# Whole-tensor loads and whole chunks for every batch of a gated recurrence and its mixer

## The chip, the cores and the metric

One core of a Trainium2 chip runs the kernel. The metric is the device time of one execution in microseconds; the number quoted for a kernel is the median of its runs.

## The reference

Four batches, eight heads, a sequence of 768 and a head size of 48; all inputs and the output are float32. First a gated linear recurrence for each batch and head:

```python
for t in range(S):
    state = alpha[:, :, t, :, None] * state + np.einsum('bhd,bhe->bhde', k[:, :, t], v[:, :, t])
    y[:, :, t] = np.einsum('bhd,bhde->bhe', q[:, :, t], state)
```

Its result, with the heads side by side (x of 768 x 384 for each batch), goes through a mixer of low rank along the sequence, and then through an MLP of width 1536:

```python
h = xt @ U @ V                     # xt: x transposed; U 768x32, V 32x768
u = x + h.transpose(0, 2, 1)
ch = np.maximum(u @ w_ch1, 0.0) @ w_ch2
return (u + ch)
```

The mixer mixes over the whole sequence. So the MLP of a batch can begin only when the recurrence of that batch is complete.

## The kernel before

**The recurrence in chunks.** The sequence of a batch is cut into pieces of 128 rows, the partitions. For each piece the kernel takes the logarithm of alpha (`lt`, on ACT), sums it along the rows by a matmul with a triangular matrix (`f_cum`), takes the exponent of the sum with either sign (`ai`, `aa`, `tot`), scales k and q by these (`rk`, `rq`; `f_scale`), transposes both on TensorE (`f_tr`) and evacuates them (`kT`, `qT`; `f_ev`), multiplies them into scores (`f_sc`), masks these (`pm`; `f_mask`), and forms y from the masked scores and `rv` (v in bf16) and from `qT` and the state that the pieces before have left (`f_y`). The state itself is carried on by `f_d`, an addition and `f_st`.

**Two layouts.** Batch 3 is done by `stage_gla`: a piece is a chunk of 128 consecutive positions of all eight heads, and there are six of them. The batches in `PAIR = (0, 1, 2)` are done by `stage_pair`: a piece is 256 positions of four heads, in which a partition holds two neighbouring positions. That makes the contiguous pieces of a load 2 x 48 floats, 384 B, where a chunk of batch 3 has 48 floats, 192 B. In a pair unit the sums take two more matmuls (L385, L386), and scores, states and y are made in halves of 64 rows (L445, L479, L531), so with more and smaller matmuls. `stage_pair` may put `f_scale` on DVE or on POOL, `stage_gla` on POOL only.

**Mixer and MLP.** `stage_mix` makes x times U (`utx`), adds h to x (`ub`, L713) and makes the transposed `uT`; `mlp1` (L749) makes `h1` from `uT` and the first weights, in two halves of the sequence; `mlp2` (L772) makes the output of a chunk from `h1` and the second weights; DVE adds `ub` (L779) and SP stores 192 KB (L780).

**Loads.** All transfers are issued by SP, in one queue. `load` in `stage_loads` brings 192 KB at a time (L342 for pairs, L349 for chunks of batch 3), into one of 36 buffers of the pool `io`, which the 24 tiles of float32 weights (L317, then cast to bf16 on POOL or ACT) use too. `U` and `V` have places of their own.

**Order.** No engine chooses at run time: the class `Plan` collects all operations with what they read and write, the engines that can do them, a cost in ns and a priority, and plays them through once while the program is being built. Out of that comes the order in which each engine's queue is written. A load has a cost for SP (750 for a pair tile, 1000 for a chunk, 540 for a weight tile). A buffer (`Buf`) takes a slot of its pool when its first operation is placed and gives it back after its last. The priority of a load is that of its batch and chunk (`b * NC + c` and a small offset); the first weights have 5.5, the second `W2AT = 7.9`. Operations of the recurrence have `(b * NC + c) * 100` and a few more, and those of the MLP of a batch come about three chunks after the recurrence of the next has begun (`mlp_prio`). While TensorE waits during the first 28 us of the plan, matmuls on zeros are put in (`P.warm`, "filler").

Of the kernel before, what the change touches and what calls it, by code (L numbers as in the profile page):

```python
# [8 lines left out]
FP32 = mybir.dt.float32  # L9
BF16 = mybir.dt.bfloat16  # L10
AF = mybir.ActivationFunctionType
# [3 lines left out]
class Pool:  # L15

    def __init__(self, slots):
        self.slots = list(slots)
        self.free = [0.0] * len(self.slots)


class Buf:
# [10 lines left out]
    def __call__(self):  # L33
        return self.slot
# [140 lines left out]
def mm(*cols):  # L175
    return sum(max(c / 2.4 + 2.5, 25.0) for c in cols)
# [3 lines left out]
def kernel(  # L180
# [24 lines left out]

    const = ctx.enter_context(tc.tile_pool(name="const", bufs=1))
# [15 lines left out]
    u_sb = const.tile([128, NC, R], BF16, name="u_sb")  # L222
    vm_sb = const.tile([128, S], BF16, name="vm_sb")
# [23 lines left out]
    sel = const.tile([R, 4, R], BF16, name="sel")  # L247
# [48 lines left out]
    def copy(eng, dst, src):  # L296
        if eng == "ACT":
            nc.scalar.copy(dst, src)  # L298
        elif eng == "DVE":
            nc.vector.tensor_copy(dst, src)  # L300
        else:
            nc.gpsimd.tensor_copy(dst, src)  # L302

    def small():
        P.add({"SP": 450.0}, lambda e: nc.sync.dma_start(u_in, moe_U.rearrange("(c p) r -> p c r", p=128)), w=["u_in"], prio=2.5)
        P.add({"SP": 500.0}, lambda e: nc.sync.dma_start(v_in, moe_V), w=["v_in"], prio=2.5)
        P.add({"POOL": 300}, lambda e: nc.gpsimd.tensor_copy(u_sb, u_in), r=["u_in"], w=["u"], prio=395)
        P.add({"POOL": 800}, lambda e: nc.gpsimd.tensor_copy(v_bf, v_in), r=["v_in"], w=["v_bf"], prio=396)
        for i in range(2):
            vb = Buf(bank)  # L310
            sl = slice(i * TW, (i + 1) * TW)
            P.add({"PE": mm(TW)}, lambda e, vb=vb, sl=sl: nc.tensor.matmul(vb()[:, 0:TW], lhsT=sel.rearrange("r a b -> r (a b)"), rhs=v_bf[:, sl], start=True, stop=True), r=["v_bf"], w=[vb], prio=397, mode="V")
            P.add({"DVE": 470, "ACT": 390}, lambda e, vb=vb, sl=sl: copy(e, vm_sb[:, sl], vb()[:, 0:TW]), r=[vb], w=[("vm", i)], prio=398)

    def weight(dst, src, key, prio, pr, engs):
        t = Buf(io)
        P.add({"SP": 540.0}, lambda e: nc.sync.dma_start(flat(t), src), w=[t], prio=prio)  # L317
        P.add(engs, lambda e: copy(e, dst, flat(t)), r=[t], w=[key], prio=pr)

    def flat(t):  # L320
        return t().rearrange("p h d -> p (h d)")
# [12 lines left out]
    tiles = {}  # L334

    def stage_loads(b):
        def load(t, src, c, key):
            if b in PAIR:
                hs, sl = slice((c % 2) * HP, (c % 2 + 1) * HP), slice((c // 2) * 2 * C, (c // 2 + 1) * 2 * C)
                P.add(  # L340
                    {"SP": 750.0},
                    lambda e: nc.sync.dma_start(  # L342
                        t().rearrange("p (h j) d -> p h (j d)", j=2), src[b, hs, sl, :].rearrange("h (p j) d -> p h (j d)", j=2)
                    ),
                    w=[t], prio=key,
                )
                return
            sl = slice(c * C, (c + 1) * C)
            P.add({"SP": 1000.0}, lambda e: nc.sync.dma_start(t(), src[b, :, sl, :].rearrange("h t d -> t h d")), w=[t], prio=key)  # L349

        for c in range(NC):
            at, qt, kt, vt = (Buf(io) for _ in range(4))
            tiles[b, c] = at, qt, kt, vt
            kk = b * NC + c
            for t, src, o in ((at, alpha, -0.7 if c else 0.0), (kt, k, 0.1), (qt, q, 0.2), (vt, v, 1.25 if c < NC - 1 and b in PAIR else 0.3)):
                load(t, src, c, kk + o)

    def xk(b, xb, c):
        return [(xb, c, 0), (xb, c, 1)] if b in PAIR else [(xb, c)]

    def stage_pair(b, u, sprev, xb):

        blk, half = u // 2, u % 2
        pr = (b * NC + u) * 100.0
        sl = 0.0 if b == 0 else 150.0
        at, qt, kt, vt = tiles[b, u]

        def raw(t):
            return t().rearrange("p (h j) d -> p j h d", j=2)

        def jh(x):
            return x.rearrange("p (j h) d -> p j h d", j=2)

        lt = Buf(lts)
        P.add({"ACT": 435}, lambda e: nc.scalar.activation(jh(lt()[:, :, 0:D]), raw(at), AF.Ln), r=[at], w=[lt], prio=pr + 40, slack=sl)  # L375
        rv = Buf(rvs)
        P.add({"POOL": 480, "ACT": 420}, lambda e: copy(e, jh(rv()), raw(vt)), r=[vt], w=[rv], prio=pr + 20, slack=sl)

        cb = Buf(bank)
        Q = HP * D  # L380
# [16 lines left out]
        aa, ai, tot = Buf(aas), Buf(ais), Buf(tots)  # L397
# [10 lines left out]
        P.add(both, lambda e: f_scale(e, rk, kt, ai), r=[kt, ai], w=[rk], prio=pr + 10, slack=sl)  # L408
        P.add(both, lambda e: f_scale(e, rq, qt, aa), r=[qt, aa], w=[rq], prio=pr + 11, slack=sl)

        tk, tq = Buf(bank), Buf(bank)
        kT, qT = Buf(kts), Buf(qts)
# [54 lines left out]
        def sview(x):  # L467
            return x[0]()[:, 2 * x[1] : 2 * x[1] + 2, :].rearrange("p a d -> p (a d)")
# [20 lines left out]
        for c in range(nch):  # L489
# [14 lines left out]
            else:  # L504
# [3 lines left out]
                    lambda e, c=c, sm=sm, prev=prev: nc.vector.tensor_tensor(sm()[:, 0:Q], db[c]()[:, 0:Q], sview(prev), op=ALU.add),  # L508
                    r=[db[c], prev], w=[sm], prio=pr + 4, slack=sl,
# [31 lines left out]
    def stage_gla(b, c, sprev, xb):  # L541
        kk = b * NC + c
        pr = kk * 100.0
        sl = 150.0
        at, qt, kt, vt = tiles[b, c]
        lt = Buf(lts)
        P.add({"ACT": 435}, lambda e: nc.scalar.activation(lt()[:, :, 0:D], at(), AF.Ln), r=[at], w=[lt], prio=pr + 40, slack=sl)
        rv = Buf(rvs)
        P.add({"POOL": 480}, lambda e: copy(e, rv(), vt()), r=[vt], w=[rv], prio=pr + 20, slack=sl)

        cb = Buf(bank)

# [11 lines left out]
        aa, ai, tot = Buf(aas), Buf(ais), Buf(tots)  # L564
# [10 lines left out]
        P.add(both, lambda e: f_scale(e, rk, kt, ai), r=[kt, ai], w=[rk], prio=pr + 10, slack=sl)  # L575
        P.add(both, lambda e: f_scale(e, rq, qt, aa), r=[qt, aa], w=[rq], prio=pr + 11, slack=sl)

        tk, tq = Buf(bank), Buf(bank)
        kT, qT = Buf(kts), Buf(qts)
# [41 lines left out]
        if c < NC - 1:  # L621
# [25 lines left out]
            else:  # L647
# [4 lines left out]
                    r=[db, sprev], w=[sm], prio=pr + 4, slack=sl,  # L652
# [112 lines left out]
    def mlp2(b, ub, h1, c):  # L765
# [13 lines left out]
        P.add({"DVE": 468}, lambda e: nc.vector.tensor_tensor(ou(), ub()[:, c, :], hb()[:, 0:DM], op=ALU.add), r=[hb, (ub, c)], w=[ou], prio=-100)  # L779
        P.add({"SP": 550.0}, lambda e: nc.sync.dma_start(out[b, c * C : (c + 1) * C, :], ou()), r=[ou], prio=-1)  # L780

    small()
    weights1()
    weights2()
    for b in range(B):
        stage_loads(b)
    for b in range(B):
        xb, ub, uT, h1 = Buf(xbs), Buf(ubs), Buf(uts), Buf(h1s)
        st = [None, None]
        for c in range(NC):  # L790
            if b in PAIR:
                st[c % 2] = stage_pair(b, c, st[c % 2], xb)
# [40 lines left out]
```

## Time and profile before

| | |
|---|---|
| median of 3 runs | 176.6 us (176.31, 176.6, 178.05) |
| span of the profiled execution | 175.2 us |
| between that span and the runs shown | 1.1 to 2.8 us, 1.4 at the median |
| TensorE busy | 165.0 us, 94% |
| DVE, ACT, POOL busy | 116.8, 104.9, 52.9 us |
| bytes moved | 28.84 MB |
| granted TensorE clock | 1.000 |

The profile is that of one execution. Its span runs from the first to the last instruction; a run's time has the start and the end of the program besides, so the execution profiled has 175.2 us of span and, by the runs, one to three us around it. "Busy" is the time in which an engine had an instruction in work; matmuls overlap, so a busy TensorE need not be at its peak. The chain of waits follows the last instruction back to what released it, step by step, and so tells which work, or which transfer, the end hung on. A window's line gives busy times of the engines in a stretch of the span, then the granted clock, the share of the 16 DMA engines and the bandwidth.

### The profile page before, as it was taken

How to read it: one execution, taken by the hardware profiler on the slowest of the kernel's cores; microseconds unless marked ns; L12 is line 12 of the kernel's file. 1: busy time of each engine (PE TensorE's matmuls, PEld its weight loads, DVE VectorE, ACT ScalarE, POOL GpSimd, SP SyncE). 2: the span in 40 equal slices, each digit the busy share in tenths (PEclk: the TensorE clock that was granted, in tenths of full speed). 3: DMA queues.
4: the chain of work that ended last, by engine and by line, in shares of the span. 5: the costliest groups of instructions: out<-in, count | busy, mean ns of one | idle time of the engine just before them, and what ended most of it. 6: DMA issues, size and time to landing. Idle time of an engine off the chain costs nothing.

```text
span 175.2 us, 5094 instructions
## 1 busy us (share of the span) xinstructions
PE 165.0 (94%) x1990; PEld 104.8 (60%) x1990; DVE 116.8 (67%) x251; ACT 104.9 (60%) x248; POOL 52.9 (30%) x92
## 2 busy tenths in 40 slices
PE   7788998699999999999999999999999999999992
PEld 2455665366566775766666666766666566666660
DVE  4588785398998889979888649987373385000321
ACT  4588874678788966457677434647784110996000
POOL 8055366258234432233243242920331000000000
PEclk9999999999999999999999999999999999999999
DMA  5999999999999999999698991021000212100222
GB/s 131 275 248 258 256 277 329 256 300 329 272 258 269 256 283 282 272 175 242 151 202 141 206 178 46 4 89 45 4 0 0 95 45 90 51 0 0 90 90 90
DMA packets 70744, 28.84 MB, mean 165 GB/s; under 512 B 64544, under 2 KB 70688, under 8 KB 70720
## 3 DMA queue, kind: packets, MB, share of 16 engines
q1 hardware_dynamic: 70720, 28.52, 67.2%
q8 instruction: 15, 0.25, 0.6%
q14 instruction: 9, 0.07, 0.2%
HBM read 23.79 MB, written 4.72 MB: 163 GB/s over the span
## 4 chain that ended last, share of the span: by engine, by line
PE 62%; SPq 14%; DMA 14%; POOL 4%; issue 3%; DVE 0%; POOLq 0%
PE ps L772 25%; PE ps L749 21%; SPq L342 11%; DMA io<-in_moe_w_ch_dram 6%; DMA io<-in_v_dram 5%; DMA io<-in_k_dram 3%; SPq L317 3%; POOL w_sb L302 2%; PE ps L418 2%; PE ps L712 2%; PE ps L722 2%; PE ps L584 2%; PE ps L531 1%; PE ps L445 1%; PE ps L605 1%
## 5 line engine op out<-in xcount | busy, mean ns | idle before, releaser
L749 PE MATMUL ps<-uT,w_sb 128*128 128x384 bf16 x288 | 53.5, 326 | 0.0
L772 PE MATMUL ps<-w_sb,h1t 128*128 128x384 bf16 x288 | 52.9, 326 | 0.0
L759 ACT ACTIVATE h1t<-ps 128x384 bf16<-128x384 f32 x70 | 33.9, 492 | 12.0 <-PE ps L749 11.9
L772 PEld LDWEIGHTS <-h1t 128*128 128x128 bf16 x288 | 26.1, 98 | 15.5 <-issue 0.6
L749 PEld LDWEIGHTS <-w_sb 128*128 128x128 bf16 x288 | 25.9, 98 | 15.4
L779 DVE TENSOR_TENSOR ou<-ub,ps 128x384 f32<-128x384 bf16 x24 | 13.2, 551 | 26.0 <-PE ps L772 25.8
L456 DVE TENSOR_TENSOR pm<-ps,maskp 128x512 bf16<-128x512 f32 x36 | 23.5, 682 | 2.8 <-PE ps L445 2.5
L761 DVE TENSOR_SCALAR h1t<-ps 128x384 bf16<-128x384 f32 x26 | 14.1, 553 | 7.6 <-PE ps L749 4.6
L302 POOL CAST rv<-io 128x384 bf16<-128x384 f32 x17 | 9.6, 567 | 28.2 <-DMA io<-in_v_dram 21.5
L298 ACT CAST xb<-ps 128x192 bf16<-128x192 f32 (+1 forms) x26 | 8.8, 353 | 10.3 <-PE ps L664 5.9
L298 ACT COPY qt<-ps 128x512 bf16<-128x512 bf16 x18 | 12.8, 709 | 3.5 <-PE ps L418 3.3
L375 ACT ACTIVATE lt<-io 128x384 bf16<-128x384 f32 x18 | 9.5, 527 | 8.3 <-DMA io<-in_alpha_dram 5.5
L713 DVE TENSOR_TENSOR ub<-xb,ps 128x384 bf16<-128x384 bf16 x24 | 12.0, 547 | 1.3 <-PE ps L712 1.3
L572 POOL TENSOR_TENSOR rk<-io,ai 128x384 bf16<-128x384 f32 x6 | 5.8, 970 | 22.6 <-ACT ai L565 22.6
L302 POOL CAST w_sb<-io 128x384 bf16<-128x384 f32 x21 | 10.6, 517 | 4.7 <-DMA io<-in_moe_w_ch_dram 4.4
L405 POOL TENSOR_TENSOR rk<-io,ai 128x384 bf16<-128x384 f32 x8 | 7.3, 915 | 11.6 <-ACT ai L398 10.8
L398 ACT ACTIVATE ai<-ps 128x384 bf16<-128x384 f32 x18 | 8.8, 487 | 2.1 <-PE ps L391 1.9
L298 ACT COPY kt<-ps 128x512 bf16<-128x512 bf16 x14 | 8.2, 583 | 1.8 <-PE ps L584 1.7
L615 DVE TENSOR_TENSOR pm<-ps,maskc 128x512 bf16<-128x512 f32 x12 | 7.9, 684 | 1.9 <-PE ps L605 1.8
L399 ACT ACTIVATE aa<-ps 128x384 bf16<-128x384 f32 x18 | 8.9, 493 | 0.0
L405 DVE TENSOR_TENSOR rk<-io,ai 128x384 bf16<-128x384 f32 x10 | 5.9, 588 | 4.1 <-ACT ai L398 4.1
L298 ACT COPY uT<-ps 128x768 bf16<-128x768 bf16 x4 | 3.2, 799 | 8.5 <-PE ps L722 8.3
(112 smaller groups left out, 256.8 us busy)
## 6 DMA issues: line engine op xcount, KB each, us to landing
io<-in_alpha_dram SPq DMA_DIRECT2D x24, 192.0 KB, 4.5
io<-in_k_dram SPq DMA_DIRECT2D x24, 192.0 KB, 4.5
io<-in_q_dram SPq DMA_DIRECT2D x24, 192.0 KB, 4.5
io<-in_v_dram SPq DMA_DIRECT2D x24, 192.0 KB, 4.6
io<-in_moe_w_ch_dram SPq DMA_DIRECT2D x24, 192.0 KB, 4.2
out_dram<-ou SPq DMA_DIRECT2D x24, 192.0 KB, 1.9
u_in<-in_moe_U_dram SPq DMA_DIRECT2D x1, 96.0 KB, 4.5
v_in<-in_moe_V_dram SPq DMA_DIRECT2D x1, 96.0 KB, 4.5
```

What stands on the lines that cost most here:

```text
L298: nc.scalar.copy(dst, src)
L302: nc.gpsimd.tensor_copy(dst, src)
L342: lambda e: nc.sync.dma_start(t().rearrange("p (h j) d -> p h (j d)", j=2), src[b, hs, sl, :].rearrange("h (p j) d -> p h (j d)", j=2)),
L375: P.add({"ACT": 435}, lambda e: nc.scalar.activation(jh(lt()[:, :, 0:D]), raw(at), AF.Ln), r=[at], w=[lt], prio=pr + 40, slack=sl)
L405: eng.tensor_tensor(jh(dst()[:, :, 0:D]), raw(a), jh(x()), op=ALU.mult)
L456: nc.vector.tensor_tensor(dst, s2, maskp.to_broadcast([C, 2, 2, C]), op=ALU.mult)
L713: P.add({"DVE": 465}, lambda e, c=c, hb=hb: nc.vector.tensor_tensor(ub()[:, c, :], xb()[:, c, :], hb()[:, 0:DM], op=ALU.add), r=[hb] + xk( ...
L749: nc.tensor.matmul(hb()[:, 0:TW], lhsT=w1_sb[:, ct, jt * 128 : (jt + 1) * 128], rhs=uT()[:, ct, tt * TW : (tt + 1) * TW], start=(ct == 0), ...
L759: nc.scalar.activation(dst, hb()[:, 0:TW], AF.Relu)
L761: nc.vector.tensor_scalar_max(dst, hb()[:, 0:TW], 0.0)
L772: nc.tensor.matmul(hb()[:, 0:DM], lhsT=h1()[:, jt, c * C : (c + 1) * C], rhs=w2_sb[:, jt, :], start=(jt == 0), stop=(jt == NJ - 1),)
L779: P.add({"DVE": 468}, lambda e: nc.vector.tensor_tensor(ou(), ub()[:, c, :], hb()[:, 0:DM], op=ALU.add), r=[hb, (ub, c)], w=[ou], prio=-100)
```

## The change

All four batches are done by `stage_gla` (`PAIR` is empty). Each of the sixteen input tensors (alpha, k, q, v of four batches) comes in one load of 1.18 MB, into one of eight large buffers: a partition gets, for each head and each of the six chunks, the 48 floats of one position, heads outside, chunks inside. A chunk is then a strided view (`Chunk`) of four large buffers. The weights and `U` and `V` use sixths of the same buffers (`Part`); `V` comes in two halves. `stage_loads(0)` is called before the small tensors and the weights, and all four loads of a batch have its first chunk's priority. The pools of `xb`, `ub` and `uT` have two buffers each and not three. `stage_pair` stays in the file, unused. The compute of a whole chunk is that of batch 3 before.

```diff
-    PAIR = (0, 1, 2)
+    PAIR = ()
...
-    v_in = const.tile([R, S], FP32, name="v_in")
...
-    io = Pool(slots("io", 36, [C, H, D], FP32))
+    bigs = Pool(slots("big", 8, [C, NC * DM], FP32))
...
-    xbs = Pool(slots("xb", 3, [128, NC, DM], BF16))
-    ubs = Pool(slots("ub", 3, [128, NC, DM], BF16))
+    xbs = Pool(slots("xb", 2, [128, NC, DM], BF16))
+    ubs = Pool(slots("ub", 2, [128, NC, DM], BF16))
     utxs = Pool(slots("utx", 2, [128, DM], BF16))
-    uts = Pool(slots("uT", 3, [128, NCT, S], BF16))
+    uts = Pool(slots("uT", 2, [128, NCT, S], BF16))
...
+    class Part:
+
+        def __init__(self):
+            if Part.used % NC == 0:
+                Part.big = Buf(bigs)
+            self.big, self.i = Part.big, Part.used % NC
+            self.key = (self.big, self.i)
+            Part.used += 1
+
+        def __call__(self):
+            return self.big()[:, self.i * DM : (self.i + 1) * DM]
+
+    class Chunk:
+
+        def __init__(self, big, c):
+            self.big, self.c, self.key = big, c, big
+
+        def __call__(self):
+            return self.big().rearrange("p (h c d) -> p h c d", h=H, c=NC)[:, :, self.c, :]
...
+            P.add({"SP": 250.0}, lambda e, i=i, sl=sl: nc.sync.dma_start(v2[i]()[0:R, 0:TW], moe_V[:, sl]), w=[v2[i].key], prio=2.5)
+            P.add({"POOL": 400}, lambda e, i=i, sl=sl: nc.gpsimd.tensor_copy(v_bf[:, sl], v2[i]()[0:R, 0:TW]), r=[v2[i].key], w=[("v_bf", i)], prio=396)
...
     def weight(dst, src, key, prio, pr, engs):
-        t = Buf(io)
-        P.add({"SP": 540.0}, lambda e: nc.sync.dma_start(flat(t), src), w=[t], prio=prio)
+        t = Part()
+        P.add({"SP": 540.0}, lambda e: nc.sync.dma_start(t(), src), w=[t.key], prio=prio)
...
+        def whole(t, src, key):
+            P.add(
+                {"SP": 4300.0},
+                lambda e: nc.sync.dma_start(
+                    t().rearrange("p (h c d) -> p h c d", h=H, c=NC), src[b].rearrange("h (c p) d -> p h c d", p=C)
+                ),
+                w=[t], prio=key,
+            )
...
+        bb = []
+        for i, src in ((0, alpha), (2, k), (1, q), (3, v)):
+            bb.append((i, Buf(bigs)))
+            whole(bb[-1][1], src, b * NC + 0.01 * len(bb))
+        bb = dict(bb)
         for c in range(NC):
-            at, qt, kt, vt = (Buf(io) for _ in range(4))
-            tiles[b, c] = at, qt, kt, vt
+            tiles[b, c] = [Chunk(bb[i], c) for i in range(4)]
...
+    stage_loads(0)
     small()
+    Part.used += -Part.used % NC
     weights1()
     weights2()
-    for b in range(B):
+    for b in range(1, B):
         stage_loads(b)
```

More of the change, by code (lines that the diff above doesn't have):

```diff
@@ L302, in copy @@
             nc.gpsimd.tensor_copy(dst, src)
-    def small():
[L305 to L308, printed above, removed]
+    class Part:
[7 more added lines that the diff above has]
+            return self.big()[:, self.i * DM : (self.i + 1) * DM]
+    Part.used = 0
+    class Chunk:
[3 more added lines that the diff above has]
+            return self.big().rearrange("p (h c d) -> p h c d", h=H, c=NC)[:, :, self.c, :]
+    def small():
+        ui, vi = Part(), Part()
+        vj = Part()
+        v2 = [vi, vj]
+        P.add({"SP": 450.0}, lambda e: nc.sync.dma_start(ui()[:, 0 : NC * R].rearrange("p (c r) -> p c r", c=NC), moe_U.rearrange("(c p) r -> p c r", p=128)), w=[ui.key], prio=2.5)
+        P.add({"POOL": 300}, lambda e: nc.gpsimd.tensor_copy(u_sb, ui()[:, 0 : NC * R].rearrange("p (c r) -> p c r", c=NC)), r=[ui.key], w=["u"], prio=395)
         for i in range(2):
@@ L311, in small @@
             sl = slice(i * TW, (i + 1) * TW)
-            P.add({"PE": mm(TW)}, lambda e, vb=vb, sl=sl: nc.tensor.matmul(vb()[:, 0:TW], lhsT=sel.rearrange("r a b -> r (a b)"), rhs=v_bf[:, sl], start=True, stop=True), r=["v_bf"], w=[vb], prio=397, mode="V")
+            P.add({"SP": 250.0}, lambda e, i=i, sl=sl: nc.sync.dma_start(v2[i]()[0:R, 0:TW], moe_V[:, sl]), w=[v2[i].key], prio=2.5)
+            P.add({"POOL": 400}, lambda e, i=i, sl=sl: nc.gpsimd.tensor_copy(v_bf[:, sl], v2[i]()[0:R, 0:TW]), r=[v2[i].key], w=[("v_bf", i)], prio=396)
+            P.add({"PE": mm(TW)}, lambda e, vb=vb, sl=sl: nc.tensor.matmul(vb()[:, 0:TW], lhsT=sel.rearrange("r a b -> r (a b)"), rhs=v_bf[:, sl], start=True, stop=True), r=[("v_bf", i)], w=[vb], prio=397, mode="V")
             P.add({"DVE": 470, "ACT": 390}, lambda e, vb=vb, sl=sl: copy(e, vm_sb[:, sl], vb()[:, 0:TW]), r=[vb], w=[("vm", i)], prio=398)
     def weight(dst, src, key, prio, pr, engs):
-        t = Buf(io)
-        P.add({"SP": 540.0}, lambda e: nc.sync.dma_start(flat(t), src), w=[t], prio=prio)
-        P.add(engs, lambda e: copy(e, dst, flat(t)), r=[t], w=[key], prio=pr)
-    def flat(t):
-        return t().rearrange("p h d -> p (h d)")
+        t = Part()
+        P.add({"SP": 540.0}, lambda e: nc.sync.dma_start(t(), src), w=[t.key], prio=prio)
+        P.add(engs, lambda e: copy(e, dst, t()), r=[t.key], w=[key], prio=pr)
     def weights1():
@@ L337, in load @@
         def load(t, src, c, key):
[L338 to L347, printed above, removed]
@@ L348, in load @@
-            sl = slice(c * C, (c + 1) * C)
-            P.add({"SP": 1000.0}, lambda e: nc.sync.dma_start(t(), src[b, :, sl, :].rearrange("h t d -> t h d")), w=[t], prio=key)
-        for c in range(NC):
-            at, qt, kt, vt = (Buf(io) for _ in range(4))
-            tiles[b, c] = at, qt, kt, vt
-            kk = b * NC + c
-            for t, src, o in ((at, alpha, -0.7 if c else 0.0), (kt, k, 0.1), (qt, q, 0.2), (vt, v, 1.25 if c < NC - 1 and b in PAIR else 0.3)):
-                load(t, src, c, kk + o)
+            hs, sl = slice((c % 2) * HP, (c % 2 + 1) * HP), slice((c // 2) * 2 * C, (c // 2 + 1) * 2 * C)
@@ new lines, in load @@
+            P.add(
+                {"SP": 750.0},
+                lambda e: nc.sync.dma_start(
+                    t().rearrange("p (h j) -> p h j", j=2 * D), src[b, hs, sl, :].rearrange("h (p j) d -> p h (j d)", j=2)
+                ),
+                w=[t.key], prio=key,
+            )
+        def whole(t, src, key):
+            P.add(
+                {"SP": 4300.0},
+                lambda e: nc.sync.dma_start(
+                    t().rearrange("p (h c d) -> p h c d", h=H, c=NC), src[b].rearrange("h (c p) d -> p h c d", p=C)
+                ),
+                w=[t], prio=key,
+            )
@@ new lines, in stage_loads @@
+        if b in PAIR:
+            for c in range(NC):
+                kk = b * NC + c
+                tiles[b, c] = [None] * 4
+                for i, src, o in ((0, alpha, -0.7 if c else 0.0), (2, k, 0.1), (1, q, 0.2), (3, v, 1.25 if c < NC - 1 else 0.3)):
+                    t = Part()
+                    tiles[b, c][i] = t
+                    load(t, src, c, kk + o)
+            return
+        bb = []
+        for i, src in ((0, alpha), (2, k), (1, q), (3, v)):
+            bb.append((i, Buf(bigs)))
+            whole(bb[-1][1], src, b * NC + 0.01 * len(bb))
@@ L368, in raw @@
         def raw(t):
-            return t().rearrange("p (h j) d -> p j h d", j=2)
+            return t().rearrange("p (h j d) -> p j h d", j=2, d=D)
         def jh(x):
@@ L374, in stage_pair @@
         lt = Buf(lts)
-        P.add({"ACT": 435}, lambda e: nc.scalar.activation(jh(lt()[:, :, 0:D]), raw(at), AF.Ln), r=[at], w=[lt], prio=pr + 40, slack=sl)
+        P.add({"ACT": 435}, lambda e: nc.scalar.activation(jh(lt()[:, :, 0:D]), raw(at), AF.Ln), r=[at.key], w=[lt], prio=pr + 40, slack=sl)
         rv = Buf(rvs)
-        P.add({"POOL": 480, "ACT": 420}, lambda e: copy(e, jh(rv()), raw(vt)), r=[vt], w=[rv], prio=pr + 20, slack=sl)
+        P.add({"POOL": 480, "ACT": 420}, lambda e: copy(e, jh(rv()), raw(vt)), r=[vt.key], w=[rv], prio=pr + 20, slack=sl)
         cb = Buf(bank)
@@ L407, in stage_pair @@
         both = {"DVE": 420, "POOL": 885}
-        P.add(both, lambda e: f_scale(e, rk, kt, ai), r=[kt, ai], w=[rk], prio=pr + 10, slack=sl)
-        P.add(both, lambda e: f_scale(e, rq, qt, aa), r=[qt, aa], w=[rq], prio=pr + 11, slack=sl)
+        P.add(both, lambda e: f_scale(e, rk, kt, ai), r=[kt.key, ai], w=[rk], prio=pr + 10, slack=sl)
+        P.add(both, lambda e: f_scale(e, rq, qt, aa), r=[qt.key, aa], w=[rq], prio=pr + 11, slack=sl)
         tk, tq = Buf(bank), Buf(bank)
@@ L546, in stage_gla @@
         lt = Buf(lts)
-        P.add({"ACT": 435}, lambda e: nc.scalar.activation(lt()[:, :, 0:D], at(), AF.Ln), r=[at], w=[lt], prio=pr + 40, slack=sl)
+        P.add({"ACT": 435}, lambda e: nc.scalar.activation(lt()[:, :, 0:D], at(), AF.Ln), r=[at.key], w=[lt], prio=pr + 40, slack=sl)
         rv = Buf(rvs)
-        P.add({"POOL": 480}, lambda e: copy(e, rv(), vt()), r=[vt], w=[rv], prio=pr + 20, slack=sl)
+        P.add({"POOL": 480}, lambda e: copy(e, rv(), vt()), r=[vt.key], w=[rv], prio=pr + 20, slack=sl)
         cb = Buf(bank)
@@ L574, in stage_gla @@
         both = {"POOL": 885}
-        P.add(both, lambda e: f_scale(e, rk, kt, ai), r=[kt, ai], w=[rk], prio=pr + 10, slack=sl)
-        P.add(both, lambda e: f_scale(e, rq, qt, aa), r=[qt, aa], w=[rq], prio=pr + 11, slack=sl)
+        P.add(both, lambda e: f_scale(e, rk, kt, ai), r=[kt.key, ai], w=[rk], prio=pr + 10, slack=sl)
+        P.add(both, lambda e: f_scale(e, rq, qt, aa), r=[qt.key, aa], w=[rq], prio=pr + 11, slack=sl)
         tk, tq = Buf(bank), Buf(bank)
```

## The prediction

> **What bounds the kernel now.** I read the page first, then the chain of waits, then the windows of the DMA queue, then the timeline of TensorE. The page:
>
> ```profile
> span 175.2 us, 5094 instructions
> PE 165.0 (94%) x1990; PEld 104.8 (60%) x1990; DVE 116.8 (67%) x251; ACT 104.9 (60%) x248; POOL 52.9 (30%) x92
> ...
> DMA  5999999999999999999698991021000212100222
> GB/s 131 275 248 258 256 277 329 256 300 329 272 258 269 256 283 282 272 175 242 151 202 141 206 178 46 4 89 45 4 0 0 95 45 90 51 0 0 90 90 90
> ```
>
> TensorE is busy all along, but so is the DMA for the first 23 of 40 slices, some 100 us. Which of the two sets the end is told by the chain of waits, here around 62 us and at the end:
>
> ```profile
> 56.72 4.87 DMA io<-in_v_dram
> 61.71 0.52 POOL rv L302
> 62.27 0.24 PE ps L479 x3
> ...
> 148.35 11.70 PE ps L749 x72
> 160.05 11.71 PE ps L772 x72
> 171.79 0.56 DVE ou L779
> ```
>
> Up to 62.27 us the end hangs on loads: a chunk of v of batch 1 lands at 61.6, is cast on POOL, and frees TensorE. From there the chain is TensorE alone up to 171.8, and 3.4 us of last addition and store follow. So the kernel has two halves: a DMA stream up to a last gate, then a full TensorE. The end is gate + what TensorE still has to do + 3.4 us. Both halves can be priced.
>
> **Price of the stream.** The bandwidth by window (busy columns of the engines, granted clock, DMA share, GB/s last):
>
> ```profile
> 22.00:28.00 6.00, 5.33 (x106) 3.53 (x106) 4.83 (x11) 3.37 (x9) 4.48 (x9) 1.00 0.96 304
> 12.00:20.00 8.00, 6.89 (x151) 4.87 (x152) 6.40 (x17) 6.91 (x19) 3.82 (x7) 1.00 1.18 257
> 80.00:83.00 3.00, 3.00 (x41) 2.02 (x40) 2.75 (x5) 2.47 (x8) 1.42 (x2) 1.00 1.09 242
> 88.00:92.00 4.00, 4.00 (x52) 2.46 (x54) 3.34 (x7) 2.81 (x8) 1.89 (x3) 1.00 1.25 201
> 96.00:100.00 4.00, 4.00 (x51) 2.54 (x50) 2.56 (x6) 1.84 (x4) 0.80 (x2) 1.00 1.26 207
> 97.00:102.00 5.00, 5.00 (x72) 3.18 (x71) 2.46 (x5) 2.14 (x6) 1.92 (x3) 1.00 1.34 195
> ```
>
> Each load here has 192 KB, yet the rate differs by the length of the contiguous piece: weights (1536 B pieces, 22 to 28 us) 304 GB/s, or 0.647 us each; pair tiles (384 B, 12 to 20 us) 257 GB/s, 0.765 us; chunks of batch 3 (192 B, 88 to 102 us) 195 to 207, mean 201 GB/s, 0.98 us. Only where the queue had been empty shortly before, or where stores with long pieces are in between (80 to 83 us), does a window with 192 B pieces show 242. A check: by 61.6 us, 55 pair tiles, 24 weight tiles and the two small tensors had come; 55 x 0.765 + 24 x 0.647 + 1.0 (192 KB) + 2.9 for the start (first issue 0.74, and 3.6 when the first tile landed, less its 0.77, is 2.1 of latency) makes 61.5. So the stream never paused, and its price is known to 0.1 us.
>
> **Price of TensorE.** Matmuls overlap, so I take the distance from one start to the next in the timeline:
>
> ```profile
> 107.16 0.33 PE L554 MATMUL ps<-lt,ut_ones 128*128 128x384 bf16 x1
> 107.32 0.17 PE L555 MATMUL ps<-offd,ident 128*128 128x8 bf16 x1
> 107.35 0.24 PE L557 MATMUL ps<-ones,lt 128*128 128x2 bf16 x4
> 107.45 0.32 PE L554 MATMUL ps<-lt,ut_ones 128*128 128x384 bf16 x1
> ...
> 110.02 0.33 PE L628 MATMUL ps<-rv,rk 128*128 128x96 bf16 x4
> 110.19 0.39 PE L584 MATMUL ps<-ident,rk 128*128 128x128 bf16 x4
> 110.41 0.36 PE L664 MATMUL ps<-rv,pm 128*128 128x48 bf16 x8
> 110.61 0.81 PE L772 MATMUL ps<-w_sb,h1t 128*128 128x384 bf16 x4
> ```
>
> A cumulative sum (L554 to L557) costs 0.29, a state update (L628) 0.17, four transposes 0.22, the y of a chunk 0.17 + 0.20, its scores 0.33 (the same way, 105.83 to 106.16), an MLP matmul 0.1625 (72 in 11.70). Priced so, what stands in the program of before from the L479 at 62.27 on is 109.5 us, and 62.27 to 171.8 is 109.5. The prices are good.
>
> **The change part by part.**
>
> *Less TensorE work.* A pair unit costs 2.05 us, a whole chunk 1.6 (sums of such rows). Without the filler the program goes from 148.8 to 141.8 us; 5.2 of the 7.0 saved lie behind the first MLP matmul (133.8 before, 128.6 after). This is the gain.
>
> *Half as long pieces for batches 0 to 2.* The destination view has `(h c d)`, the source `h (c p) d`: each partition takes 48 pieces of 192 B. One whole load is 1.18 MB. What it costs (call it w) no row shows; bounds: 1.18 MB at 257 GB/s is 4.59 us, the pace of pieces twice as long; at 195 GB/s 6.05. A full queue of 192 B pieces is what a stream of whole loads is, so I take the three full rows, 201 GB/s: w = 5.87 us, against 6 x 0.765 = 4.59 before.
>
> The Trainium skill, page "DMA: Bandwidth & Descriptors", has a rule for this change (section "Measured": make DMAs 1 MiB or larger) and one against it (section "Why small descriptors are slow": some 3 cycles on top of each packet's 32 B beats). The rows above, all of equal size, go with piece length. By the second rule two pieces take 18 cycles where one of 384 B takes 15; as an estimate w = 5.51 and a time of 189; by the first rule's 341 GB/s, w = 3.46, and the stream would not set the end. No run here shows a 1.18 MB load yet.
>
> *Order on SP.* All of batch 0 (4 w), U and V (1.0), first weights (12 x 0.647 = 7.8), all of batch 1 (4 w), second weights (7.8), batch 2 (4 w), batch 3 with five stores before its last load. The eight big buffers are reused long after their readers are done (first reuse is batch 1's k in alpha 0's place, at some 41 us; the Ln of batch 0 are through by some 15), so no load waits. If one did, all behind it on SP would be late by as much.
>
> *The gates.* In the trace TensorE's instructions start in the order of the program, and the changed program puts the consumers of each load at a fixed place in it. For each I add landing time, 0.7 us (61.6 to 62.27, as before), the work left and 3.4:
> - alpha of batch 1: its fourth cumulative sum stands ahead of the first MLP matmul. 2.9 + 1.0 + 7.8 + 5 w = 41.0; four Ln of 0.52 and the sum, 2.4; 128.6 left: 175.4. That alone eats the gain.
> - v of batch 1: 58.7 + 0.7 + 119.2 + 3.4 = 182.0.
> - v of batch 2: 2.9 + 1.0 + 15.5 + 12 w = 89.8. The first L664 of batch 2 stands early, when only 36 of the 288 second MLP matmuls and 72 of the first are done. Behind it: 468 MLP matmuls, 76.05; 12 of L748, 1.95; 42 of L758 at 0.056, 2.35; nine cumulative sums, 2.6; 20 x 0.22, 4.5; 11 scores, 3.6; ten updates and ten state terms, 3.4; 12 x 0.20, 2.4; 12 of L717, 0.9: together 97.75. 89.8 + 0.7 + 97.75 + 3.4 = 191.7.
> - v of batch 3: 12 w + 4 w and five stores of 0.65: 116.6 + 0.7 + 68.5 + 3.4 = 189.2.
>
> The latest is v of batch 2. Span 191.7; runs were 176.31 to 178.05 for a span of 175.2, the median 1.4 over it: **193.1 us**.
>
> *Costed at nothing.* POOL alone scales k and q now (12 x 0.92 a batch, and six casts of 0.50, 13.9 us): it hides under the 23.5 us of a batch's loads, all but what follows v. Without that cover up to 5 casts and 5 scales, 7 us, come behind the gate, beside MLP work. Two xb, ub and uT: batch 2 needs batch 0's places, whose MLP then is what TensorE is doing; uncovered, it costs at most one block of 72 matmuls, 11.7. More filler (33 for 14) runs only where TensorE waits; the granted clock is 1.00 in all windows anyway. 80 fewer issues on SP save nothing on a stream that is never short of issues.
>
> **The rivals.**
> - *The stream keeps up and the lighter chunks win.* Break-even is a landing of v of batch 2 at 175.2 - 101.85 = 73.35, so w = 4.50, 262 GB/s. For it: the plan in the code prices a pair tile 750 and a small chunk 1000 ns, close to my 765 and 980, and a whole load at 4300; if that too is as good, w = 4.3, the landing 71.0, the span 172.9, time 174.3. Against: no window of 192 B pieces reaches it. Chance 0.13, of it 0.06 within 1%.
> - *The rate of an unfilled queue holds throughout*, 242 GB/s: w = 4.87, landing 77.8, span 179.7, time 181. For it: a window shows it; against: it held only for some us. Chance 0.2.
> - *The gate is right and TensorE starves behind it*, because POOL's 7 us or DVE's masks feed batch 2 too slowly: 193 and up to 7, so 197 to 200. Against: 36 to 72 MLP matmuls lie between. Chance 0.12.
> - That the change doesn't do what it says can be excluded: the built program has 16 such loads on SP.
>
> **How the numbers follow.** My forecast (w 5.4 to 6.05, times 187.5 to 195) has 0.55; the rivals 0.13, 0.2 and 0.12. The range runs from 178 to 200. Faster by over 1% 0.07, within 1% (about what a measurement of this kernel can tell from no change) 0.06, slower 0.87.
>
> **What would show it.** Right: 192 B pieces at some 200 GB/s without pause up to about 116 us; v of batch 2 landing near 90; a TensorE row with holes between 45 and 90 us and none behind; the chain leaving DMA for good at that load. Wrong: whole loads landing 4.3 to 4.5 us apart, or a chain that ends its DMA part at batch 0 or 1.

## The result and the profile after

| | before | after |
|---|---|---|
| median | 176.84 us (four runs, 176.31 to 178.05) | 212.2 us (four runs, 211.41 to 212.91) |
| ratio | 1 | 1.1976 [1.192, 1.2031] |
| span of the profiled execution | 175.2 us | 211.1 us |
| mean granted clock | 1.000 | 0.902 |

The kernel is slower by a fifth. Ratios, here and below, compare only runs in the faster of the two states that executions show; one run of the stores experiment and three of the last but one kernel were in the slower. The forecast was 193.1 us and its range ended at 200: the side was right, the size was not. Some 19 of the 35 us lost were not foreseen. The page of the changed kernel (a slice is 5.28 us):

```profile
span 211.1 us, 4134 instructions
...
PE   7467689258884997666999933999999999999993
...
PEclk9995558757998899889999996699999999999999
DMA  5999989989999979989998891011110012210132
GB/s 119 186 186 186 187 163 342 209 175 188 191 173 278 276 156 188 190 167 201 191 197 181 195 203 32 26 52 40 56 58 0 0 40 75 75 40 0 37 112 75
```

Three things differ from before. The DMA row is full for 24 of 40 slices, now up to 127 us and not 100, mostly at 160 to 210 GB/s where the row of before mostly showed 240 to 330. The TensorE row has holes up to slice 18 (100 us), and, after four full slices, two slices of 3 around 121 to 132 us, which I had not expected at all. The clock row, whose mean was 1.000 before, falls to 0.5 in slices 3 to 5 and in slice 8, and to 0.6 in slices 24 and 25, in or behind such holes.

The chain of waits, where it leaves the last load, and at its end (start, duration, what):

```profile
118.73 8.92 DMA big<-in_v_dram
...
128.24 0.96 POOL rv L301 x2
129.20 0.88 POOL rk L608
130.12 0.61 PE ps L620 x4
130.73 1.28 PE ps L808 x4
...
184.17 11.70 PE ps L785 x72
195.87 11.71 PE ps L808 x72
```

The shape is that of before: a load of v, a cast on POOL, then TensorE to the end. But the load is v of batch **3**, not of batch 2, and between the cast and TensorE stands a scaling of k (`rk`, L608), and it is that of the last chunk of batch 2, as shown further down. TensorE then runs for 77 us behind the gate.

Windows around that gate (length, busy PE, PEld, DVE, ACT, POOL, granted clock, DMA share, GB/s):

```profile
16.00:22.00 6.00, 4.49 (x27) 2.33 (x27) 1.27 (x3) 1.47 (x3) 3.51 (x4) 0.50 1.12 187
...
98.80:123.20 24.40, 24.34 (x264) 16.20 (x263) 17.62 (x33) 15.45 (x38) 7.55 (x12) 1.00 0.95 197
123.20:130.10 6.90, 0.19 (x2) 0.00 (x0) 0.56 (x1) 0.22 (x1) 2.31 (x5) 0.89 0.66 122
128.70:135.40 6.70, 5.28 (x28) 2.81 (x30) 0.42 (x1) 1.74 (x4) 2.85 (x6) 0.50 0.01 2
```

Line 2 is TensorE behind the gate I had named (v of batch 2): full, and at full clock. Line 3 is the new hole: two matmuls in 6.9 us. Line 4 is what follows it: the clock is 0.50 while TensorE is at work, so its matmuls take twice as long (four of the MLP 1.28 us, not 0.65). Line 1 shows the same clock early, where TensorE only waits for batch 0.

The landings of the sixteen whole loads in the trace (alpha, k, q, v of each batch): 9.7, 16.03, 22.34, 28.94; 44.78, 51.43, 57.57, 63.98; 78.39, 85.25, 91.89, 98.19; 105.14, 112.38, 119.73, 127.65 us. The nine distances within batches 0 to 2 have a mean of **6.47 us**; I had w = 5.87, and the plan in the code prices 4.3.

### The profile page after: what moved, and what is told of

The parts are those of the page before. It is cut to its first block, busy times and chain, and to the rows that moved or that the text cites. A ratio compares the mean times of both kernels' runs of the same rounds, so it can differ in the third digit from the quotient of the medians.

```text
span 211.1 us, 4134 instructions
## 1 busy us (share of the span) xinstructions
PE 172.3 (82%) x1617; PEld 107.0 (51%) x1617; DVE 108.2 (51%) x213; ACT 96.8 (46%) x228; POOL 70.5 (33%) x114
## 4 chain that ended last, share of the span: by engine, by line
PE 49%; DMA 21%; SPq 18%; POOL 5%; issue 5%; DVE 1%; ACT 0%; POOLq 0%; DVEq 0%
PE ps L808 21%; PE ps L785 15%; SPq L371 13%; DMA big<-in_q_dram 6%; DMA big<-in_alpha_dram 5%; DMA big<-in_v_dram 4%; DMA big<-in_moe_w_ch_dram 4%; SPq L329 3%; PE ps L620 2%; POOL rq L608 2%; SPq L341 2%; POOL rk L608 2%; DMA out_dram<-ou 2%; PE ps L641 2%; PE ps L590 1%
## 5 line engine op out<-in xcount | busy, mean ns | idle before, releaser
L808 PE MATMUL ps<-w_sb,h1t 128*128 128x384 bf16 x288 | 55.5, 338 | 0.0
L608 POOL TENSOR_TENSOR rk<-big,ai 128x384 bf16<-128x384 f32 x24 | 22.2, 937 | 56.0 <-ACT ai L601 25.4
L808 PEld LDWEIGHTS <-h1t 128*128 128x128 bf16 x288 | 27.0, 100 | 17.3 <-issue 2.3
L651 DVE TENSOR_TENSOR pm<-ps,maskc 128x512 bf16<-128x512 f32 x48 | 31.1, 683 | 3.6 <-PE ps L641 3.6
L815 DVE TENSOR_TENSOR ou<-ub,ps 128x384 f32<-128x384 bf16 x24 | 13.3, 553 | 29.8 <-PE ps L808 29.5
L608 POOL TENSOR_TENSOR rq<-big,aa 128x384 bf16<-128x384 f32 x24 | 21.9, 923 | 11.0 <-ACT ai L601 5.7
L583 ACT ACTIVATE lt<-big 128x384 bf16<-128x384 f32 x24 | 11.8, 532 | 22.3 <-DMA big<-in_alpha_dram 15.5
L620 PE MATMUL ps<-ident,rk 128*128 128x128 bf16 x96 | 10.4, 238 | 12.6 <-POOL rk L608 12.6
L301 POOL CAST rv<-big 128x384 bf16<-128x384 f32 x24 | 11.9, 518 | 24.3 <-DMA big<-in_v_dram 14.9
L797 DVE TENSOR_SCALAR h1t<-ps 128x384 bf16<-128x384 f32 x26 | 13.9, 554 | 9.1 <-PE ps L785 8.7
L297 ACT CAST xb<-ps 128x384 bf16<-128x384 f32 x20 | 9.6, 478 | 18.5 <-PE ps L700 18.4
L620 PEld LDWEIGHTS <-rk 128*128 128x128 bf16 x96 | 6.8, 104 | 16.2 <-POOL rk L608 15.2
L620 PE MATMUL ps<-ident,rq 128*128 128x128 bf16 x96 | 10.5, 238 | 5.3 <-POOL rq L608 5.2
L590 PE MATMUL ps<-lt,ut_ones 128*128 128x384 bf16 x24 | 9.1, 380 | 6.0 <-ACT lt L583 5.9
L290 PE MATMUL ps<-filler 128*128 128x512 bf16 x33 | 12.6, 520 | 1.2 <-DVE filler L226 1.2
```

Of the source, the lines that this page charges most:

```text
L290: P.warm = lambda: nc.tensor.matmul(ps[:, 7, :], lhsT=filler[:, 0:128], rhs=filler, start=True, stop=True)
L620: nc.tensor.matmul(t[:, p, :], lhsT=ring()[:, 2 * p : 2 * p + 2, :].rearrange("t h w -> t (h w)"), rhs=ident, start=True, stop=True, is_tr ...
L651: nc.vector.tensor_tensor(pm()[:, :, par, :], s2, maskc.to_broadcast([C, HP, C]), op=ALU.mult)
L797: nc.vector.tensor_scalar_max(dst, hb()[:, 0:TW], 0.0)
L808: nc.tensor.matmul(hb()[:, 0:DM], lhsT=h1()[:, jt, c * C : (c + 1) * C], rhs=w2_sb[:, jt, :], start=(jt == 0), stop=(jt == NJ - 1),)
```

## The experiments

The theory to test (A in the expectations): the time comes from loads of short pieces that land later than the written order of the engines assumes, so that queues which can't change their order stand still behind them. Its rivals blame one part each, whatever the loads: whole chunks with POOL as the only engine that scales (B), the whole load as such, with one completion for six chunks (D), the stores that share SP's queue (E), and the smaller pools. The expectations say which numbers each gives.

### One part at a time: chunks, loads, pools

*Whole chunks alone.* The kernel before, all batches in `stage_gla`, with 36 small buffers and 192 KB loads:

```diff
-    PAIR = (0, 1, 2)
+    PAIR = ()
```

> The kernel before with whole chunks for all batches (PAIR empty), but with its 192 KB loads, one for each chunk, and three buffers for x and u. Theory A (the load stream sets the end: how fast it is and how late the plan's order lets it release TensorE): the pieces are 192 B, 0.98 us a load by batch 3 of before, but they come in the order of use; the latest gate (alpha of a late chunk of batch 2, landing about 87 us, 83.5 us of TensorE work left) gives a span of 178 to 179, time about 180. Theory B (the whole chunks themselves cost the time, by scaling on POOL alone): 200 or more, since that part of the change is all in here.

185.15 us, ratio 1.0386 [1.0246, 1.0527]. B falls: with the same compute and the same short pieces the loss is a fifth of the 1.1976. A's number is 5 us short; the stream is again slower than it was priced, for the last chunk of v lands at 126.4, about where the changed kernel's last v lands (127.65). Two kernels with nearly the same last landing differ by 27 us. The stream's length can't be the whole cause.

*Whole loads for batch 3 alone.* The changed kernel with pairs for the others:

```diff
-    PAIR = ()
+    PAIR = (0, 1, 2)
```

> The changed kernel with pair units and 192 KB pair loads for batches 0 to 2 again; large buffers, two buffers for x and u, and whole loads and whole chunks only for batch 3. Theory A: batch 3 comes as four whole loads of 6.45 us behind all the pair tiles, its v at about 104; with some 70 us of TensorE work left that is a span of 178 to 182, time 180 to 184. Theory B (POOL alone scales): about 177, since only batch 3 has whole chunks, as before. Theory C (fewer and larger buffers hold up the MLP): 190 or more.

186.18 us, ratio 1.0444 [1.0317, 1.0571], 2 us above the expectation. The four whole loads land at 82.5, 89.8, 97.9 and 105.4; TensorE has one hole of 4.2 us at 103.6, and half clock from 107.6 to 111. The hole ends with the scaling of a state of batch 2 (`st`, L530, at 107.32 on POOL), which stood on POOL behind four casts of v of batch 3 (from 105.51). One batch of whole loads has in small what the changed kernel has at its gate.

*Two buffers for x and u alone.* The kernel before with pools of two:

```diff
-    xbs = Pool(slots("xb", 3, [128, NC, DM], BF16))
-    ubs = Pool(slots("ub", 3, [128, NC, DM], BF16))
+    xbs = Pool(slots("xb", 2, [128, NC, DM], BF16))
+    ubs = Pool(slots("ub", 2, [128, NC, DM], BF16))
...
-    uts = Pool(slots("uT", 3, [128, NCT, S], BF16))
+    uts = Pool(slots("uT", 2, [128, NCT, S], BF16))
```

> The kernel before with two buffers each, and not three, for xb, ub and uT; nothing else. The order of all instructions is the same. If these buffers are free in time, as costed: no change, 176 to 178. Theory C (the third buffer mattered): 180 or more.

178.36 us beside 178.07, ratio 0.9988 [0.9946, 1.003]. The smaller pools cost nothing here; the prediction's zero holds.

### Long pieces

The changed kernel, but a partition takes six neighbouring positions, 1152 B in one piece. The size of a load, its single completion, the buffers and the instructions stay the same; the positions lie in another order in the chunks, so the output is that of a permuted sequence.

```diff
-                    t().rearrange("p (h c d) -> p h c d", h=H, c=NC), src[b].rearrange("h (c p) d -> p h c d", p=C)
+                    t().rearrange("p (h c d) -> p h c d", h=H, c=NC), src[b].rearrange("h (p c) d -> p h c d", p=C)
```

> The changed kernel with one thing different: each partition takes six neighbouring positions of a head, so that a whole load has the same 1.18 MB but contiguous pieces of 1152 B and not of 192 B. The positions stand in another order in the chunks, so the recurrence is computed over permuted positions; number, size and order of all instructions are the same. Theory A: a load takes about 4.0 us (295 GB/s, between the 257 of 384 B and the 304 of 1536 B pieces), the gates come at 47 to 67 us, span 173 to 175, time about 175. Theory D (a load of 1.18 MB is slow by its size, since SP can keep only one more in the queue): 6 us a load as before, time over 200.

175.58 us, ratio 0.985 [0.9729, 0.997]. The whole loss is gone, and a little of the gain from lighter chunks is left. A window of its stream (columns as above):

```profile
10.00:16.00 6.00, 4.29 (x52) 2.47 (x50) 1.80 (x5) 4.06 (x13) 5.85 (x7) 1.00 1.10 350
```

350 GB/s, against 187 in the changed kernel's window at 16 to 22 us; the loads of batch 0 land at 6.7, 10.0, 13.3 and 16.8, 3.37 us apart. D falls as a cause by itself: a load of 1.18 MB is no burden if it comes quicker than the plan's 4.3 us. The pieces of 192 B are a necessary part of the loss.

The rule of the Trainium skill, page "DMA: Bandwidth & Descriptors", section "Measured", to make DMAs 1 MiB or larger (the page's table is of loads issued from GpSimd, these are issued by SP), did not decide here: at the same 1.18 MB the rate is 187 or 350 GB/s, by the length of the piece alone.

*Is POOL short of time?* The same kernel, and DVE may scale too:

```diff
-        both = {"POOL": 885}
+        both = {"DVE": 420, "POOL": 885}
```

> The experiment with 1152 B pieces (positions permuted as there), with the scaling of k and q in a whole chunk allowed on DVE as well as on POOL. Theory B' (once the stream is out of the way, POOL's sole scaling holds up the recurrence of batch 0): the first MLP matmul, at 36.7 there, comes at 32 to 34, span 169 to 171, time 171 to 173. If POOL is hidden: 175 to 176 as there.

174.24 us, ratio 0.9803 [0.9632, 0.9975]; the first MLP matmul starts at 35.7 and not at 36.7 us. The intervals of the two kernels overlap. With the stream quick, POOL as the only engine for the scaling costs about 1 us, if anything.

### The price in the plan

The changed kernel, and only the cost by which the plan places a whole load goes from 4.3 to 6.4 us, near what it takes. The loads and the computing instructions are the same; their order changes, the stores take other places in SP's queue, and the plan puts in 48 filler matmuls where the changed kernel has 33.

```diff
-                {"SP": 4300.0},
+                {"SP": 6400.0},
```

> The changed kernel with the plan's cost of a whole load raised from 4300 to 6400 ns: the same loads, but the plan writes each engine's queue in the order that fits the measured landing times. Theory A with the order as part of the loss: v of batch 2 and 3 land at 97 and 126 as now, but less work stands behind them (POOL's k scaling of batch 3 no longer behind v); the latest gate gives 187 and with clock and other losses 191 to 195, time about 194. If the stream alone decided whatever the order: 208 or more.

192.3 us, ratio 1.0787 [1.0602, 1.0973]; in shares of the time before that is 0.119, or **21 us** (some 3.4 to either side), back for one number in the plan. The loads are no faster: v of batch 2 lands at 100.0 and v of batch 3 at 128.2, both a little later than in the changed kernel. What TensorE has done by then is told by three windows of each kernel (first the changed kernel, then this one):

```profile
0.00:50.00 50.00, 33.52 (x306) 19.30 (x307) 22.71 (x51) 19.84 (x50) 25.17 (x52) 0.73 0.98 194
50.00:100.00 50.00, 38.00 (x395) 24.05 (x394) 30.87 (x61) 26.19 (x64) 22.70 (x33) 0.93 0.96 202
100.00:128.00 28.00, 23.39 (x254) 15.32 (x250) 17.41 (x33) 14.94 (x35) 6.55 (x10) 1.00 0.95 190
```

```profile
0.00:50.00 50.00, 39.17 (x356) 21.76 (x359) 25.68 (x61) 22.39 (x57) 24.87 (x52) 0.90 0.98 196
50.00:100.00 50.00, 46.05 (x492) 30.49 (x489) 33.36 (x66) 31.75 (x74) 24.41 (x32) 0.93 0.95 211
100.00:128.00 28.00, 27.67 (x309) 18.45 (x308) 20.68 (x38) 16.54 (x40) 12.75 (x17) 1.00 0.98 190
```

By 128 us TensorE has run 306 + 395 + 254 = 955 matmuls in the changed kernel, and 356 + 492 + 309 = 1157 in this one: 202 more. Which ones the second MLP line (L808, here cut off at 128 us) shows; of the first MLP line both have run 144:

```profile
L808 PE MATMUL ps<-w_sb,h1t x72: 322/326/527, 78.6 to 107.3; 128*128 128x384 bf16 x72
```

```profile
L808 PE MATMUL ps<-w_sb,h1t x144: 322/326/524, 69.2 to 127.8; 128*128 128x384 bf16 x144
```

72 of the 202 are MLP matmuls of 0.1625 us, 11.7 us, and 15 are filler, which does no work of the kernel. The other 115 are mostly small ones of the recurrence; at 0.055 us, the price of one of four transposes in the prediction, they would be some 6 us (an estimate). The half clock behind the hole cost 2.6 (see the part on the prediction). Together some 20.6, where the stretch from 128 us to the end is 211.1 - 189.3 = 21.8 us shorter. The filler, which runs in the first 28 us, is not the cause: in the changed kernel all that stands ahead of the gate was done at 123.2, and TensorE then stood still, so a slower TensorE before that cost the end nothing.

What held TensorE is seen on POOL. First the changed kernel, then the one with the right price (start, duration, idle time before):

```profile
127.80 1.40 POOL L301 CAST rv<-big 128x384 bf16<-128x384 f32 x3 [10.79 <-DMA big<-in_v_dram]
129.16 0.90 POOL L608 TENSOR_TENSOR rk<-big,ai 128x384 bf16<-128x384 f32 x1
```

```profile
103.23 0.92 POOL L608 TENSOR_TENSOR rk<-big,ai 128x384 bf16<-128x384 f32 x1
128.29 2.77 POOL L301 CAST rv<-big 128x384 bf16<-128x384 f32 x6 [0.96 <-issue]
```

Both scalings are the sixth behind the landing of k of batch 2, so those of its last chunk. With the price of 4.3 us the plan put three casts of v of batch 3 ahead of it, and it ran at 129.16; with 6.4 us it stands ahead of the casts, and it ran at 103.23. So the short price keeps ready work of older batches, on POOL and on TensorE, *behind* the consumers of a load that has not landed, in queues that run in order; the right price puts it ahead.

### One completion, or six

*Six loads instead of one.* The changed kernel, with each tensor in six loads of 192 KB into the same large buffer; a chunk's readers wait only for their sixth. Six times 717 is the 4.3 us of before.

```diff
-            self.big, self.c, self.key = big, c, big
+            self.big, self.c, self.key = big, c, (big, c)
...
-            P.add(
-                {"SP": 4300.0},
...
+            for c in range(NC):
+                P.add(
+                    {"SP": 717.0},
+                    lambda e, c=c: nc.sync.dma_start(
+                        t().rearrange("p (h c d) -> p h c d", h=H, c=NC)[:, :, c, :], src[b, :, c * C : (c + 1) * C, :].rearrange("h p d -> p h d")
+                    ),
+                    w=[(t, c)], prio=key,
+                )
```

> The changed kernel with each whole load cut into six of 192 KB, one for each chunk, in the same order, into the same large buffers; a chunk then waits for its own loads alone. The pieces stay 192 B. Theory A (piece length): six loads take 6 x 0.98 = 5.9 us, v of batch 3 lands near 112, span 192 to 198, time 194 to 199. Theory D (size: one large load is worse than six small ones by more than the row of batch 3 of before says): 4.9 us for six at the rate of an unfilled queue, time about 185. If only piece length and bytes count and the finer waiting gives nothing: 205 or more.

207.2 us, ratio 1.1658 [1.1394, 1.1922], some 10 us above the expectation. A window of its stream:

```profile
5.00:20.00 15.00, 9.78 (x82) 5.20 (x82) 2.83 (x14) 7.75 (x21) 6.50 (x8) 0.83 1.41 187
```

187 GB/s again, and over the same nine distances six loads take 6.59 us on average against 6.47 for one: the size of a load hardly matters to the rate. The expectation had the finer completion as the larger part of the cure. It isn't, as long as the plan is written for 4.3 us.

*Six loads and the price near what they take:*

```diff
-                    {"SP": 717.0},
+                    {"SP": 1040.0},
```

> The experiment with six loads of 192 KB in place of each whole load, with one number changed: the plan's cost of such a load is 1040 ns, as they landed there, and not 717. Loads, order of loads, bytes and pieces are the same. Theory F (the stream's length alone does not make the loss; the queues were written for a stream that is a third faster): work behind the last gate falls from 73 to 54 us, the gates give 176.3, with 4 to 8 us of losses as elsewhere a span of 180 to 184, time 182 to 186. If the length of the stream alone sets the end: 203 or more, as there.

184.55 us, ratio 1.0391 [1.0334, 1.0448]: 0.127 of the time before, or 22 us, for the price alone, as with whole loads. The last v lands at 127.0, no earlier than with the short price (125.8). The order of the tensors' loads on SP is the same; a few buffers and the places of stores shift, so the step is not of a single number only. The second MLP line (L809 in these two) up to 128 us, first with 717, then with 1040:

```profile
L809 PE MATMUL ps<-w_sb,h1t x80: 323/326/528, 79.0 to 127.0; 128*128 128x384 bf16 x80
```

```profile
L809 PE MATMUL ps<-w_sb,h1t x144: 322/326/337, 65.0 to 122.0; 128*128 128x384 bf16 x144
```

The same sign as before: 64 of these matmuls had been left for later. And 184.55 is where the loads by chunk of the first experiment are (1.0386 and 1.0391): loading by tensor costs nothing that these runs show, if it completes in six parts and is priced near what it takes. Between this kernel and the one with the right price and whole loads, 1.0787 - 1.0391 makes 0.040, 7 us, with an interval of some 3.4 us to either side: that is what one completion for six chunks costs. The other way round, with the short price, it is 1.1976 - 1.1658 = 0.032, 6 us, with an interval of some 5. So the price is worth 21 or 22 us and the completion 6 or 7, whichever is changed first.

### The stores

The changed kernel, with the stores issued by ACT:

```diff
-        P.add({"SP": 550.0}, lambda e: nc.sync.dma_start(out[b, c * C : (c + 1) * C, :], ou()), r=[ou], prio=-1)
+        P.add({"ACT": 60.0}, lambda e: nc.scalar.dma_start(out[b, c * C : (c + 1) * C, :], ou()), r=[ou], prio=-1)
```

> The changed kernel with the 24 stores of the output issued from ACT's queue and not from SP's, so that no load stands behind a store on SP. Theory E (part of the loss is v of batch 3, which stood on SP behind stores that could be issued only when the load before had drained): v of batch 3 is issued with the queue and lands near 120 and not at 127.65; span some 203, time 204 to 206. If the stores on SP cost nothing: 211 to 213.

212.03 us (two runs, 210.34 and 213.72, the second profiled): no gain near the 7 us that E expected, though a gain of some 2 us can't be told from none. Its chain of waits shows why:

```profile
112.75 14.97 DMA big<-in_v_dram
...
128.32 1.41 POOL rv L301 x3
```

The last v lands at 127.7, as with the stores on SP (127.65). It was issued at 112.75 and not at 118.73, 6 us earlier, and came no sooner. E falls: standing behind stores on SP is not what makes the last load late. What stays open is why v of batch 2 landed 2.7 us later here (100.89 against 98.19), and the four loads behind it took 26.8 us against 29.5.

### Versions that might beat both

Only batches whose loads are not what TensorE waits for can afford short pieces. So the kernel before, with pairs for the first two batches only:

```diff
-    PAIR = (0, 1, 2)
+    PAIR = (0, 1)
```

> The kernel before with whole chunks for batch 2 as well as 3 (PAIR = (0, 1)), by its own 192 KB chunk loads. Theory A: batch 2's loads come when the stream is ahead of TensorE, so their 24 x 0.28 us more are hidden, and TensorE has 2.7 us less to do: 174 to 176 where before has 177 to 178. If 192 B pieces cost time wherever they are: 179 or more.

175.11 us, ratio 0.9866 [0.983, 0.9903]: a little faster than both kernels. Batch 2 in whole chunks saves TensorE 6 x (2.05 - 1.6) = 2.7 us by the prediction's prices; the ratio makes 2.4 us.

The same, and DVE may scale in whole chunks (the edit of the long-pieces kernel above):

> The same with the scaling of k and q in whole chunks allowed on DVE too. If POOL's sole scaling holds up batches 2 and 3: some 1 us less than without, 173 to 175. If it is hidden: the same.

175.13 us (174.94 over the nine runs that count in the ratio), ratio 0.9842 [0.9809, 0.9874]. The intervals overlap: no difference that these runs show. And with pairs for batch 0 only, DVE scaling too:

> Whole chunks for batches 1 to 3, by 192 KB chunk loads, scaling on DVE or POOL; only batch 0 in pairs. Theory A: batch 1's loads are on the stream that sets the pace up to some 70 us; 24 x 0.28 = 6.7 us of stream more against 2.7 us less of TensorE work: the gates give 173.2, time 176 to 180, slower than with batches 0 and 1 in pairs. If only batch 0 needs its loads early: 172 to 174.

177.63 us, ratio 1.0018 [0.999, 1.0047]. With batch 1 in short pieces the gain is gone, as expected from a longer stream; no run separates the parts.

## Why the prediction was right in its side and wrong in its size

**What held.** "Gate + what TensorE still has to do + 3.4 us" describes the changed kernel too. The prices of TensorE hold: from 98.86 us on, where the first L664 of batch 2 starts, to the hole at 123.2, the work priced at 23.9 us took 24.3; behind 137.7 us, two stretches priced at 26.7 and 42.1 took 27.3 and 42.6. The gate of v of batch 2 behaves as told: the load lands at 98.19, TensorE goes on 0.67 later (0.7 in the sum), with 97.75 left. Alone it would have ended the span at 98.86 + 97.75 + 3.4 = 200.0, and the only error in it would have been the landing (89.8 in the sum).

**The step that failed is the gate of v of batch 3.** The sum gave it 116.6 + 0.7 + 68.5 + 3.4 = 189.2 and so put it behind batch 2's. It ended at 211.1, 21.9 us later, from four terms:

| term | in the sum | measured | more |
|---|---|---|---|
| landing of v of batch 3 | 116.6 | 127.65 | 11.05 |
| from there to TensorE | 0.7 | 2.47 | 1.8 |
| work left at this gate, at the sum's prices | 68.5 | 73.8 | 5.3 |
| what TensorE took over those prices | 0 | 3.8 | 3.8 |

- *The landing.* w was 6.47 and not 5.87; sixteen times 0.6 is 9.6 of the 11. No row of before showed a whole load, and the prediction said so. The three windows of before that I priced from, 195 to 207 GB/s, were not the floor of such a stream. By the second rule the prediction named (the Trainium skill, page "DMA: Bandwidth & Descriptors", section "Why small descriptors are slow") the estimate was 5.51, further off than the row.
- *The lag and the work left* are one omission: POOL's queue. I costed POOL "at nothing" behind the gate but for at most 7 us "beside MLP work" (its sum for a batch, 13.9 us, is 14.0 by its own terms). The waits of TensorE in the changed kernel (us, times, longest):

```profile
PE ps L620 <- POOL rk L608: 12.6, 4, 6.7
```

  The longest of these, 6.7 us, is the hole. What TensorE lacks there is the transposes (L620) of the last chunk of *batch 2*, whose k had landed at 85.25 and whose `ai` was ready at 121.6. In POOL's order three casts of v of batch 3 (L301) stand ahead of its scaling of k, so POOL waits for a load of the next batch, and TensorE with it; then the three casts (1.40) and the scaling (0.90) pass before it can go on at 130.12. That it is batch 2's last chunk is told by the count of the scalings and by what comes next: x times U of batch 2, which needs all six chunks of x, starts only behind it:

```profile
139.41 0.50 PE L717 MATMUL ps<-xb,u_sb 128*32 128x384 bf16 x6
```

  These transposes stand earlier in TensorE's queue than the L664 of batch 3 that I had taken as the first victim, so 5.3 us more are left behind them. Had the scaling stood ahead of the casts, the 5.3 us of work up to that L664 would have lasted from 123.4 to some 128.7, past the landing at 127.65 and one cast, and there would have been next to no hole (an estimate from these rows; no run changed this order alone). The prediction followed TensorE's queue from the gate, and not the queue of the engine that feeds it. The expectation of the right price named POOL too, but took the scaling for one of batch 3.
- *The clock.* "The granted clock is 1.00 in all windows anyway" was true of a kernel whose TensorE hardly paused. From 130.12 to 137.7 us work priced at 5.0 took 7.58, and the clock there was 0.50: 2.6 of the 3.8. No run took the half clock away alone, either. The Trainium skill, page "TensorE: Matmul & The Clock Gate", Part 1, has the rule: half clock after an idle window of some 3.4 us, full clock again after a busy one, with windows that run freely, whatever the kernel does. The hole of 6.9 us and the 0.50 behind it agree. The clock came back 5.3 us after TensorE's first matmul here and 3.1 us after it in the kernel with whole loads for batch 3 alone, which fits windows that don't start with the work.

**The zeros that held:** the smaller pools (0.9988), the stores' place in SP's queue (no clear gain on ACT), and POOL's sole scaling where the stream is quick (about 1 us).

**The rivals.** "The stream keeps up" had taken the plan's 4.3 us as a sign of the load's real time. The opposite is so: that number, 2.2 us below what a load takes, is the largest part of the loss. "The rate of an unfilled queue" falls with 187 GB/s. "TensorE starves behind the gate" came true in part, by POOL's order and the clock, and at the gate of batch 3's v, not the one it named.

**What the 35 us are made of**, by the differences of ratios: short pieces for all batches, net of the lighter chunks, 0.039 or 7 us (192 KB loads by chunk, and the six priced loads); one completion for six chunks 0.040 or 7 us; an order written for 4.3 us a load 0.119 or 21 us. They come from different comparisons, with intervals of some 1, 3.4 and 3.4 us to either side. All three need the short pieces: with 1152 B pieces they are gone together.

## What to carry to other kernels

Price a load by the length of its contiguous pieces, not by the size of the DMA; and where a static order is written from such prices, put the measured one in before anything else is judged, for here the wrong price cost three times what the slower loads themselves did. When costing a gate, walk the queue of every engine between the load and the engine that sets the end, and ask what stands *ahead* of the first needed instruction there. Short-piece layouts pay in the batches whose loads have slack: with batch 2 beside batch 3 the kernel gets 1.3% faster, with all of them 20% slower.

## What the runs showed of the hardware

The size of a load hardly shows in the rate: 192 B pieces came at 187 GB/s in loads of 192 KB and of 1.18 MB alike. What does show is how long SP is held while it issues. The loads of k and q in the changed kernel and then with long pieces (duration of the issue in ns, least, median, largest; starts from and to):

```profile
L371 SPq DMA_DIRECT2D big<-in_k_dram x4: 697/6274/7817, 2.1 to 103.3; - x4
L371 SPq DMA_DIRECT2D big<-in_q_dram x4: 696/5651/5852, 7.5 to 111.0; - x4
```

```profile
L371 SPq DMA_DIRECT2D big<-in_k_dram x4: 418/547/579, 1.2 to 65.4; - x4
L371 SPq DMA_DIRECT2D big<-in_q_dram x4: 398/2612/3764, 1.8 to 69.5; - x4
```

In a run of whole loads SP is held for about as long as a load takes to come: 6.3 and 5.7 us at the median with short pieces (a load comes every 6.47), and up to 3.8 us with pieces of 1152 B (every 3.37). With short pieces the second load of a batch (k) is already held; with long ones the second is issued in 0.55 us, and only the third (q) is held. And it is not the load's own issue that is long, for a store of 192 KB that stands behind whole loads is held just so, where the median store takes 0.33 us:

```profile
97.23 5.84 SPq L816 DMA_DIRECT2D out_dram<-ou  x1
```

Issued by ACT, in the experiment on stores, every one of the 24 stores took 0.34 to 0.37 us, while SP was held at its loads as before. So the hold fell on the engine that had issued the loads, and not on another.
